# A scheduler that counts visits of small matrix products later, and copies that may go to either of two engines

## The chip, the cores and the metric

The kernel runs on one core of a Trainium2 chip. The metric is the device time of one execution in microseconds (us). The engines are TensorE (PE, with its weight loads as PEld), VectorE (DVE), ScalarE (ACT), GpSimd (POOL) and SyncE (SP, which issues the transfers). TensorE runs at one of two clocks, 1.2 or 2.4 GHz; the profile calls the granted clock 0.50 or 1.00.

## What is computed

An attention with a state that is updated token by token (batch 4, 8 heads, 768 tokens, head size 48), followed by two feed-forward layers over 3072 tokens of width 384:

```python
k_n = k / (norm(k) + 1e-6)
for t in range(S):                      # S = 768
    y[t] = q[t] @ state
    state = state + beta[t] * outer(k_n[t], v[t] - k_n[t] @ state)
x = y as 3072 x 384
x = ((x @ w_a) * (x @ w_b)) @ w_out     # width 1536
h = x @ w_in                            # width 2048
out = (max(h, 0) + alpha * min(h, 0)) @ w_out2
```

## The kernel before, in words

The attention works on six chunks of 128 tokens (c = 0 to 5), each of two steps of 64 tokens (j = 0, 1). For a chunk, small products on TensorE make the grams of keys and queries (tile `g`), VectorE inverts a triangular matrix in a long row of small operations (`inv`, `itmp`), two more stages of small products complete the inverse (`w`, and `xx` in the first chunk), and each step is then a chain: `rp` (what the state already holds), a subtraction on VectorE, `up`, copies of `up` into `SU`, `sp`, the new state from `sp`, and `yp`, the output. ScalarE and VectorE split `yp` into a high and a low half in `x`, from which the large products of the feed-forward layers start (`p` and `o` in the first layer, `h` and `o` in the second, each 128x512). The small products are fp32, and so each counts as two TensorE instructions in the trace; the large ones use split fp32r operands, three passes each.

Nothing is issued in the order of the Python code. A `Recorder` notes every operation, a `Schedule` lays them out, and `emit` issues them in that order; the trace therefore shows line 203 for all of them. `Schedule.run` is a list scheduler. It keeps a planned time `free` for each engine and `ready` for each task; consecutive small products form one task, each large product is a task of its own. At each turn it takes the engine that can start first, and on it the task of highest `level` among those that can start within `SLACKS` of that time (0.25 us on TensorE). The plan fixes the order on every engine; the true times follow from the chip. `plan` makes four such runs with different levels and keeps the one whose planned end is earliest.

"The front" is all that TensorE does ahead of the first large product. There, gaps in TensorE's plan are filled with dummy products, `spin`, 128x512 each, that depend on nothing but a cleared tile; `spins` lists them and gets a `None` once the first large product is placed. The inner loop puts in spins from the end of the last task while this holds:

```python
each = SPIN if fast(at) else 2 * SPIN          # SPIN = 0.227
if at + each > b - REST - 0.08 * (b - free[e]) or len(spins) == len(s.spins):
    break                                      # REST = 0.25, 200 spins at hand
```

where `b` is the planned start of the next task. Their number is thus fixed when the kernel is built, and on the chip TensorE goes through all of them before it comes to the product behind them, whether that product's operands are there or not. An operation recorded on `nc.evict` may go to ScalarE or VectorE: ScalarE is tried first, and VectorE takes it where ScalarE's plan is more than `BUSY` = 1.5 us behind, or where it is the earlier by the plan (the function `when`).

The first chunk's copies of `up` into `SU` (in `step`, lines 960 to 965) go to ScalarE for x = 0 and to VectorE for x = 1; in later chunks all of them go to ScalarE. Both copies of one half read the same PSUM tile.

Of the kernel before, what the change touches and what calls it, by code (L numbers as in the profile page):

```python
# [125 lines left out]
PE_, ACT_, DVE_, POOL_, SP_ = range(5)  # L126
# [76 lines left out]
            getattr(s.engines[op.eng], name)(*(real(x) for x in op.a), **{w: real(x) for w, x in op.k.items()})  # L203


HOP, SAME, LATE, BEGIN = 0.15, 0.03, 1.0, 1.3
ENTER, LEAVE = 0.2, 0.19
BUSY = 1.5
TURNS = 4
# [35 lines left out]
class Schedule:  # L245
# [105 lines left out]
    def run(s, level):  # L351

        tasks = s.tasks
        waits = [len(t.before) for t in tasks]
        ready, start, end = ([0.0] * len(tasks) for _ in range(3))
        open_ = [[t.n for t in tasks if not waits[t.n] and any(w[0] == e for w in t.ways)] for e in range(5)]
        free, port, link, was = [BEGIN] * 5, 0.0, 0.0, False
        rows = [None] * 5
        landed, order, spins = [], [], []
        chunk, spans = {"at": 0, "next": 0.0}, []  # L360
        clock = {"w": 0, "fast": False}
        warm = s.of[min(s.spins[0].before)]

        def fast(b):
            while (clock["w"] + 1) * WINDOW <= b:
                w = clock["w"]
                busy = sum(k * (min(y, (w + 1) * WINDOW) - max(x, w * WINDOW)) for x, y, k in spans if y > w * WINDOW and x < (w + 1) * WINDOW)
                spans[:] = [x for x in spans if x[1] > (w + 1) * WINDOW]
                clock["fast"] = busy >= WINDOW * (KEEP_UP if clock["fast"] else RISE)
                clock["w"] = w + 1  # L370
            return clock["fast"]

        def ask(b):
            chunk["next"] = b + next(x for y, x in FETCH if link > b + y)

        def fetched(b, cost, n):
            at, late = chunk["at"], 0.0
            for x in range(at, at + n):
                if x == STOCK - CHUNK:
                    ask(b)  # L380
                if x >= STOCK and (x - STOCK) % CHUNK == 0:
                    now = b + late + cost * (x - at) / n
                    late += max(0.0, chunk["next"] - now)
                    ask(max(now, chunk["next"]))
            chunk["at"] = at + n
            return late

        def when(n, e):
            at, first = max(ready[n], free[e]), tasks[n].ways[0][0]
            return at if e == first or free[first] > at + BUSY else max(at, free[first] + 0.01)  # L390

        while len(order) < len(tasks):
            at, e = min((min(when(n, e) for n in open_[e]), e) for e in range(5) if open_[e])
            n = max((n for n in open_[e] if when(n, e) <= at + SLACKS[e]), key=lambda n: (tasks[n].ways[0][0] == e, level[n], -n))
            t = tasks[n]
            for w in t.ways:
                open_[w[0]].remove(n)
                if w[0] == e:
                    t.go(w)
            order.append(n)  # L400
            b = max(ready[n], free[e])
            cost, lag = t.cost, t.lag
            if e in (ACT_, DVE_, POOL_):
                if rows[e] == t.rows:
                    b = max(ready[n], free[e] - (0.12 if e != DVE_ else 0.1))
                rows[e] = t.rows
            if t.port:
                wait = max(0.0, port - b - 0.1)
                port = b + wait + t.lag - 0.05
                cost, lag = cost + wait, lag + wait  # L410
            if e == PE_:
                if not spins or spins[-1] is not None:
                    at = max(free[e], end[warm] if end[warm] else 1e9)
                    while True:
                        each = SPIN if fast(at) else 2 * SPIN
                        if at + each > b - REST - 0.08 * (b - free[e]) or len(spins) == len(s.spins):
                            break
                        spins.append(at)
                        at += each
                        spans.append((at - each, at, 1))  # L420
                        fetched(at - each, each, 2)
                    if t.large:
                        spins.append(None)
                if t.large == was:
                    b += ENTER if not t.large else LEAVE
                    spans.append((b - 0.2, b, 1))
                was = not t.large
                if not fast(b):
                    cost += t.cost
                    lag += t.cost  # L430
                late = fetched(b, cost, 2 if t.large else 4 * len(t.ops))
                cost, lag = cost + late, lag + late
                spans.append((b, b + cost, 1 if t.large else LIGHT))
            if t.dma:
                if e == SP_:
                    if len(landed) >= 8:
                        b = max(b, landed[-8])
                    landed.append(0)
                link = max(b + 1.5, link) + lag
                end[n] = link + 0.55 + (LATE if link > 45 else 0)  # L440
                if e == SP_:
                    landed[-1] = end[n]
            else:
                end[n] = b + lag
            start[n] = b
            free[e] = b + cost
            for m in t.after:
                u = tasks[m]
                if u.before[n]:
                    r = b + 1e-6  # L450
                elif u.eng == e == PE_:
                    r = b + cost
                else:
                    r = end[n] + (SAME if u.eng == e and not t.dma else HOP)
                ready[m] = max(ready[m], r)
                waits[m] -= 1
                if not waits[m]:
                    for w in u.ways:
                        open_[w[0]].append(m)
        s.start, s.end = start, end  # L460
        for t in tasks:
            t.ops[0].eng = t.eng
        s.first = min(start[t.n] for t in tasks if t.large)
        ops = [(start[n], n, op) for n in order for op in tasks[n].ops]
        ops += [(at, 0, op) for at, op in zip((x for x in spins if x is not None), s.spins)]
        return [op.n for _, _, op in sorted(ops, key=lambda x: x[:2])]
# [90 lines left out]
class Attention:  # L557
# [50 lines left out]
    def bank(s, name, tag="chain"):  # L608
        return s.pools[tag].tile([128, 512], F32, tag=tag, name=name, bufs=BANKS[tag])
# [283 lines left out]
    def step(s, c, j, L, mates=(), joined=False, wide=False):  # L893
# [6 lines left out]
        nc, ap = s.nc, s.ap  # L900
# [3 lines left out]
        def mate():  # L904
            m = mates.pop(0) if mates else None
            return none if m is None else m()
# [3 lines left out]
        SU, SN = s.SU[st % 2], s.SU[(st + 1) % 2]  # L910
# [21 lines left out]
        if st > 0:  # L932
# [12 lines left out]
            for x in range(2):  # L945
                sl, other = slice(64 * x, 64 * x + 64), slice(64 - 64 * x, 128 - 64 * x)
                got = rp[1][other, 0 : second.stop - second.start]
# [4 lines left out]
        for group in (uneven if mates else halves,) if wide else ((h,) for h in halves):  # L952
            ups = [bank("up") for _ in group]
            beside, keep = mate()
            turned = group is uneven
            for n, i, o in dealt(group, beside):
                for x in range(2):
                    sl, at = slice(64 * x, 64 * x + 64), 64 * (x ^ n ^ turned)
                    nc.tensor.matmul(ups[n][at : at + 64, i, :], s.TT[sl, j, o, :], R[sl, o, :], start=True, stop=True)
            for n, (_, hs) in enumerate(group):  # L960
                for x in range(2):
                    at = 64 * (x ^ n ^ turned)
                    got = ups[n][at : at + 64, 0 : hs.stop - hs.start]
                    (nc.scalar if c or not x else nc.vector).copy(SU[x][64 * x : 64 * x + 64, hs, 0:48], got)
                    s.spend(ACT, 1.9)
            keep()
            yield
        for group in (halves,) if wide and not mates else ((h,) for h in halves):
# [4 lines left out]
            for i in range(8):  # L973
                for n, (o, _) in enumerate(group):
                    for x in range(2):
                        sl, at = slice(64 * x, 64 * x + 64), 64 * (x ^ n)
                        nc.tensor.matmul(sps[n][at : at + 48, i, :], bk[sl, j, o + i, :], SU[x][sl, o + i, 0:48], start=True, stop=True)
                beside(i)
            for n, (_, hs) in enumerate(group):
                for x in range(2):  # L980
                    at, old, new = 64 * (x ^ n), slice(64 - 64 * x, 112 - 64 * x), slice(64 * x, 64 * x + 48)
# [11 lines left out]
        for o, _ in halves:  # L993
            for x in range(2):
                rows, at = slice(0, (112, 128)[x]), (o // 4 + x) * 64
                for n in range(4):
                    for q in range(4):
                        kk, h, e, start, stop = s.BLOCKS[q][n]
# [15 lines left out]
def attn_moe_kernel(tc, kt, qt, kn, vn, beta, w_a, w_b, w_o, w_in, w_o2, alpha, out):  # L1014
    nc = tc.nc
    with ExitStack() as ctx:
# [383 lines left out]
        for c in range(NSC):  # L1400
# [3 lines left out]
            if c > 0:  # L1404
                N = A.load(c + 1) if c + 1 < NSC else None
                if c == 1:
                    run(moe, WAIT)
                    pools["out"] = Pool(rec, second, (p0,), 1, True)
                    going = run(moe, AHEAD) and going
# [213 lines left out]
```

## Time and profile before

| | us |
|---|---|
| median of 3 runs (lowest, highest) | 1011.08 (1008.9, 1012.37) |
| the profiled execution's own time | 1012.1 |
| its span, first to last instruction | 1010.1 |
| TensorE busy in the span | 993.7 (98%) |
| first large product starts at | 75.34 |

The profiled execution is 0.1% above the median, and 2.0 us of its time lie outside of its span. TensorE's share of 98% counts the spins as work, and the ends of products are modelled by the profile.

### The profile page before, as it was taken

The numbers are of one execution on the slowest core, as the hardware profiler recorded it, in microseconds if no ns is written. First come the engines' busy times: TensorE is split into PE (matmuls) and PEld (weight loads), VectorE is DVE, ScalarE is ACT, GpSimd is POOL, SyncE is SP. The second block draws the span as 40 slices with busy tenths as digits, with TensorE's granted clock in tenths as the row PEclk, the third lists the DMA queues.
The fourth block names the chain that finished last, engine by engine and source line by source line (L and its number), as shares of the span: only waits on it lengthen the run. The fifth ranks groups of instructions, "written<-read, shape, count | busy, mean of one in ns | idle before, by whom it ended". The sixth has DMA issues, their size and how long they took to land.

```text
span 1010.1 us, 22391 instructions
## 1 busy us (share of the span) xinstructions
PE 993.7 (98%) x9388; PEld 813.3 (81%) x9388; DVE 631.5 (63%) x1260; ACT 445.7 (44%) x804; POOL 499.0 (49%) x406
## 2 busy tenths in 40 slices
PE   8989999999999999999999999999999999999998
PEld 6777777888888788788878888888888888888886
DVE  7789997865895687678677778343343343433333
ACT  5846774454545454545578785121121221211211
POOL 4557864653565366456468875333333333333332
PEclk8889999999999999999999999999999999999999
DMA  9536432002201210000035542010020010000100
GB/s 201 210 96 230 141 89 81 32 4 65 94 1 32 65 65 1 18 18 32 16 97 167 165 133 84 1 31 32 1 63 1 1 63 0 32 1 1 32 1 31
DMA packets 27076, 61.31 MB, mean 61 GB/s; under 512 B 4320, under 2 KB 8928, under 8 KB 26976
## 3 DMA queue, kind: packets, MB, share of 16 engines
q1 hardware_dynamic: 26544, 59.50, 19.5%
q8 instruction: 73, 1.20, 0.5%
q10 hardware_dynamic: 432, 0.39, 0.1%
q14 instruction: 27, 0.22, 0.1%
HBM read 50.44 MB, written 9.44 MB: 59 GB/s over the span
## 4 chain that ended last, share of the span: by engine, by line
PE 92%; POOL 2%; DMA 2%; issue 2%; DVE 1%; ACT 0%; DVEq 0%; POOLq 0%; SPq 0%
PE o L203 33%; PE p L203 27%; PE h L203 19%; PE g L203 3%; PE yp L203 2%; DMA Z<-in_qt_dram 2%; PE spin L203 2%; PE up L203 2%; POOL W L203 2%; PE sp L203 1%; PE rp L203 1%; PE w L203 1%; POOL wu L203 1%; DVE raw L203 0%; DVE inv L203 0%
## 5 line engine op out<-in xcount | busy, mean ns | idle before, releaser
L203 PE MATMUL p<-x,wu 128*128 128x512 f32 x1296 | 318.4, 394 | 2.3 <-DVE x L203 1.5
L203 PEld LDWEIGHTS p<-x,wu 128*128 128x128 f32 x1296 | 240.1, 188 | 55.6 <-issue 3.6
L203 POOL TENSOR_TENSOR g<-neg,g 128x512 fp32r<-128x512 f32 x95 | 124.5, 1311 | 261.0 <-ACT g L203 258.5
L203 POOL TENSOR_TENSOR wu<-W,wu 128x384 fp32r<-128x384 f32 (+1 forms) x126 | 176.4, 1404 | 112.6 <-ACT wu L203 112.6
L203 DVE TENSOR_SCALAR neg<-h,al 128x512 f32<-128x512 f32 (+1 forms) x97 | 72.3, 745 | 227.9 <-PE h L203 225.2
L203 PE MATMUL o<-g,v 128*128 128x512 f32 x870 | 211.5, 388 | 0.0
L203 PE MATMUL h<-x,v 128*128 128x512 f32 x864 | 211.3, 389 | 0.0
L203 ACT CAST g<-neg 128x512 fp32r<-128x512 f32 (+1 forms) x97 | 59.7, 616 | 305.6 <-DVE neg L203 280.3
L203 PEld LDWEIGHTS o<-g,v 128*128 128x128 f32 x870 | 162.4, 188 | 33.8 <-ACT g L203 0.4
L203 PEld LDWEIGHTS h<-x,v 128*128 128x128 f32 x864 | 162.1, 188 | 33.8 <-DVE neg L203 0.2
L203 PE MATMUL o<-g,wu 128*128 128x512 f32 x648 | 163.9, 393 | 1.3 <-ACT g L203 1.1
L203 PEld LDWEIGHTS o<-g,wu 128*128 128x128 f32 x648 | 120.6, 188 | 28.3 <-ACT g L203 1.5
L203 ACT CAST wu<-W 128x768 fp32r<-128x768 f32 (+1 forms) x144 | 96.8, 676 | 57.3 <-PE p L203 38.1
L203 POOL TENSOR_TENSOR g<-a,g 128x512 fp32r<-128x512 f32 x57 | 80.0, 1403 | 56.6 <-ACT g L203 56.6
L203 ACT COPY a<-p 128x512 f32<-128x512 f32 x72 | 42.2, 587 | 95.4 <-PE p L203 66.2
L203 DVE TENSOR_TENSOR inv<-inv,itmp 128x110 f32<-128x110 f32 (+12 forms) x256 | 75.0, 293 | 8.9 <-ACT eu L203 0.9
L203 DVE SCALAR_TENSOR_TENSOR neg<-h,neg 128x512 f32<-128x512 f32 (+1 forms) x97 | 66.5, 686 | 3.3
L203 PE MATMUL g<-Z 48*64 48x64 f32 (+1 forms) x1024 | 63.3, 267 | 3.9 <-DMA Z<-in_kt_dram 1.5
L203 PEld LDWEIGHTS g<-Z 48*64 48x64 f32 x1024 | 47.8, 150 | 12.3 <-issue 4.9
L203 DVE TENSOR_TENSOR a<-p,a 128x512 f32<-128x512 f32 x59 | 40.6, 688 | 25.1 <-PE p L203 24.1
L203 DVE TENSOR_TENSOR itmp<-inv,gd 128x96 f32<-128x96 f32 (+8 forms) x150 | 40.7, 271 | 6.1 <-ACT gd L203 1.4
L203 POOL TENSOR_TENSOR f<-f,v 128x384 int32<-128x384 int32 x32 | 36.5, 1156 | 10.0 <-DVE v L203 10.0
(111 smaller groups left out, 940.6 us busy)
## 6 DMA issues: line engine op xcount, KB each, us to landing
v<-in_w_o_dram SPq DMA_DIRECT2D x16, 384.0 KB, 3.2
v<-in_w_in_dram SPq DMA_DIRECT2D x16, 384.0 KB, 3.6
Z<-in_kt_dram SPq DMA_DIRECT2D x24, 192.0 KB, 3.8
Z<-in_qt_dram SPq DMA_DIRECT2D x24, 192.0 KB, 3.8
v<-in_vn_dram SPq DMA_DIRECT2D x12, 384.0 KB, 3.2
x2d<-x2s SPq DMA_DIRECT2D x18, 256.0 KB, 2.4
xf<-x2d SPq DMA_DIRECT2D x18, 256.0 KB, 2.8
raw<-in_w_a_dram SPq DMA_DIRECT2D x11, 384.0 KB, 5.2
```

Source lines behind the costliest of these rows:

```text
L203: getattr(s.engines[op.eng], name)(*(real(x) for x in op.a), **{w: real(x) for w, x in op.k.items()})
```

## The change

Two constants are added. In the front, every task of small products gets a planned start that is 0.7 us later (`FRONT`), ahead of the loop that fills the gap with spins. Behind the first large product, a task of small products counts as ready 0.4 us later (`CARE`) when the scheduler looks for what to place next; its planned start, once it is taken, isn't changed. And the first chunk's copies of `up` for x = 1 are recorded on `evict` in place of VectorE, those for x = 0 on `evict` in place of ScalarE.

```diff
-HOP, SAME, LATE, BEGIN = 0.15, 0.03, 1.0, 1.3
+HOP, SAME, LATE, BEGIN, CARE = 0.15, 0.03, 1.0, 1.3, 0.4
+FRONT = 0.7
...
         def when(n, e):
-            at, first = max(ready[n], free[e]), tasks[n].ways[0][0]
+            late = CARE if e == PE_ and spins and spins[-1] is None and not tasks[n].large else 0.0
+            at, first = max(ready[n] + late, free[e]), tasks[n].ways[0][0]
             return at if e == first or free[first] > at + BUSY else max(at, free[first] + 0.01)
...
             if e == PE_:
+                if (not spins or spins[-1] is not None) and not t.large and at > 1:
+                    b += FRONT
                 if not spins or spins[-1] is not None:
...
                     got = ups[n][at : at + 64, 0 : hs.stop - hs.start]
-                    (nc.scalar if c or not x else nc.vector).copy(SU[x][64 * x : 64 * x + 64, hs, 0:48], got)
+                    (nc.scalar if c else nc.evict).copy(SU[x][64 * x : 64 * x + 64, hs, 0:48], got)
```

No operation is added or removed by name; the order on every engine and the number of spins are what the scheduler makes of it.

## Rows read from the trace of the kernel before

**Rows 1.** The page, busy time, share and count of each engine

```profile
PE 993.7 (98%) x9388; PEld 813.3 (81%) x9388; DVE 631.5 (63%) x1260; ACT 445.7 (44%) x804; POOL 499.0 (49%) x406
```

**Rows 2.** Busy time in stretches: length, then each engine, clock, DMA share, GB/s

```profile
0.00:75.30 75.30, 66.09 (x1422) 54.95 (x1422) 59.05 (x130) 44.99 (x79) 38.92 (x53) 0.84 0.61 168
75.30:122.60 47.30, 44.94 (x192) 35.65 (x192) 44.00 (x110) 32.50 (x45) 38.36 (x23) 1.00 0.57 190
171.20:537.60 366.40, 366.40 (x4689) 297.81 (x4689) 270.01 (x658) 196.34 (x367) 202.49 (x163) 1.00 0.13 40
```

**Rows 3.** TensorE's waits from 75 to 125 us: total, times, longest

```profile
PE p L203 <- DVE x L203: 1.5, 1, 1.5
PE o L203 <- ACT g L203: 1.1, 1, 1.1
PE p L203 <- ACT a L203: 0.9, 1, 0.9
```

**Rows 4.** Busy time in the front's two stretches at half clock

```profile
17.00:34.10 17.10, 15.02 (x205) 13.16 (x207) 15.66 (x44) 9.93 (x15) 8.06 (x12) 0.50 1.02 318
64.80:71.60 6.80, 6.80 (x140) 6.14 (x143) 4.54 (x9) 2.63 (x7) 4.67 (x3) 0.50 0.24 63
```

**Rows 5.** Timeline of TensorE, the last grams and the stage behind them

```profile
20.39 6.40 PE L203 MATMUL g<-Z 48*64 48x64 f32 x106 [0.48 <-DMA Z<-in_qt_dram]
27.46 3.04 PE L203 MATMUL g<-Z 48*64 48x64 f32 x52 [0.68 <-issue]
...
40.51 1.15 PE L203 MATMUL g<-Z 48*64 48x64 f32 x32
41.59 7.34 PE L203 MATMUL spin<-still 128*128 128x512 f32 x31
48.86 1.29 PE L203 MATMUL w<-hw,ef 32*32 32x32 f32 x128
```

**Rows 6.** Timeline of VectorE and ScalarE beside it

```profile
40.64 2.07 DVE L203 STREAM_TRANSPOSE hw<-inv 128x1024 f32<-128x1024 f32 x1
...
42.40 1.21 ACT L203 ACTIVATE Z<-g 64x512 f32<-64x512 f32 x2
...
50.22 1.78 DVE L203 COPY hw<-w 32x256 f32<-32x256 f32 x4 [5.63 <-PE w L203]
```

**Rows 7.** Timeline of TensorE, from there to the last step of the front

```profile
52.42 1.12 PE L203 MATMUL xx<-TT,hw 32*32 32x32 f32 x108 [0.59 <-issue]
...
55.88 1.60 PE L203 MATMUL up<-v,TT 64*64 64x48 f32 x47 [0.78 <-issue]
...
59.48 2.00 PE L203 MATMUL yp<-Z,SU 112*32 112x64 f32 x128
...
63.16 0.92 PE L203 MATMUL rp<-SU,Z 48*64 48x48 f32 x49 [0.95 <-issue]
...
64.93 3.65 PE L203 MATMUL up<-v,TT 64*64 64x48 f32 x64
...
70.52 2.50 PE L203 MATMUL yp<-Z,SU 112*32 112x64 f32 x128
```

**Rows 8.** The copies of `up`, 50 to 75 us: count, busy, mean ns, idle

```profile
L203 ACT COPY SU<-up 64x384 f32<-64x384 f32 x4 | 1.9, 472 | 7.7 <-PE up L203 6.3 <-DVE SU L203 1.3
L203 DVE COPY SU<-up 64x384 f32<-64x384 f32 x4 | 2.2, 561 | 1.9 <-ACT SU L203 1.9
```

**Rows 9.** Timeline of TensorE, small products between large ones

```profile
127.61 1.51 PE L203 MATMUL w<-TT,hw 32*64 32x64 f32 x64
...
130.88 1.41 PE L203 MATMUL rp<-SU,Z 48*64 48x48 f32 x64
...
511.20 1.15 PE L203 MATMUL rp<-SU,Z 48*64 48x48 f32 x64
```

**Rows 10.** Timeline of TensorE and VectorE, the second block's start

```profile
171.25 1.98 PE L203 MATMUL p<-x,wu 128*128 128x512 f32 x8
...
170.96 1.07 DVE L203 TENSOR_TENSOR x<-yp,x 128x256 fp32r<-128x256 f32 x3
```

## The prediction

> **What bounds the kernel now.** I read the page's busy shares first [rows 1]: TensorE is busy for 98% of the span, so only its work, or the time in which it lacks work, can move the end. The stretches come second [rows 2]. From 171 us to 538 us TensorE is busy without a gap, with attention and first layer together, and the second layer behind it holds no small product, so neither constant is read there. What is left is the front, 75.3 us up to the first large product at 75.34, and the stretch from there to 171 us. The spins count as busy time, so the front's 66.09 us of busy time say nothing of what it must cost. I therefore read the timeline of TensorE in the front against those of ScalarE and VectorE, one small group after the other, and asked of each: was it the operands that came last, or TensorE?
>
> At the front's widest place it was TensorE. After the last grams it runs 31 spins, from 41.59 to 48.86, and then `w` [rows 5]. `w` needs the transposed inverse `hw`, which VectorE ended at 40.64 + 2.07 = 42.71, and PSUM that ScalarE cleared of the last gram at 42.40 + 1.21 = 43.61 [rows 6]. So `w` could have begun at about 43.65, and began 5.2 us later; VectorE stood idle for 5.63 us until it came. The plan had placed these 31 spins so that they would end before `hw` was there; TensorE came to them late, because it took longer over the grams than planned.
>
> Behind `w` it is a mixture. Three groups stop in their midst for 0.59, 0.78 and 0.95 us with "issue", a wait for nothing that the profile shows [rows 7]; elsewhere the copies on ScalarE and VectorE come last by some tenths. And the clock is at 1.2 GHz from 17.0 to 34.1 and from 64.8 to 71.6 [rows 4], at an exact half of the full clock. Behind the first large product TensorE waits for 1.5, 1.1 and 0.9 us [rows 3]. Waits inside small groups don't show as idle time, since the ends of products are modelled: they show as longer groups. An undisturbed `rp` of 64 takes 1.15 us [rows 9]; the one at 130.88 takes 1.41.
>
> **FRONT, up to `w`.** Per task, 0.7 us more of planned time. Where the gap was zero, the spin rule leaves room for 0.7 - 0.25 - 0.06 = 0.39 us, which is one spin of 0.227 at full clock and none at half clock. Where there was a gap already, nearly all of the 0.7 is filled: 0.92 x 0.7 / 0.227 = 2.8 spins. A spin takes 7.34 / 31 = 0.237 us on the chip [rows 5]. That decides the sign. The planned time of `w` is set by VectorE's inverse, not by TensorE. If five gram groups that run back to back (158 products, 32 each, the first two of rows 5) each take 0.7 us of the plan and are filled with at most 0.23, the gap ahead of `w` loses 5 x 0.7 us of spins and gets 5 x 0.23 back elsewhere: -2.3 us. Against it stand `w`'s own 0.7 (+0.65 filled) and the key grams ahead of the inverse, which come one or two visits later in the plan and so move the planned inverse by 0.7 to 1.4 us (+0.65 to +1.3). I take -1.0 for the start of `w`. Bounds: it can't come more than 5.2 us earlier, since its operands aren't there, and if the grams are filled as fully as the others it comes some 3 us later.
>
> **FRONT, from `w` to the first large product.** By the code these are 15 tasks: `w` and `xx` two each, then `up`, `up`, `sp`, `sp`, `yp`, `rp`, `up`, `up`, `sp`, `sp`, `yp`. Some 8 wait in the plan and get up to 3 spins more, 7 follow another and get one: 8 x 3 x 0.237 + 7 x 0.237 = 7.3 us more work in TensorE's queue. It is a chain, so uncovered it would all be lost. Cover: the three stops of "issue", 0.59 + 0.78 + 0.95 = 2.3 us, if what they wait for comes at its own time; an estimated 1.2 us in which TensorE waits for copies ahead of a group (half of the three stops); as a choice 1.5 us, about what the 7 single spins cost, where the second half of `up` or `sp` or the `yp` runs beside the copies that the chain needs. And the clock: at 1.2 GHz `up` took 3.65 us for 64, where 47 at full clock took 1.60, or 2.2 for 64; `yp` took 2.50 against 2.00 [rows 7]; with a half-clock `sp` beside them about 2.4 us in all. The fall at 64.8 comes behind the stretch with the longest stop, 0.95 us in `rp`; more spins ahead of `rp` fill just that stretch. 2.3 + 1.2 + 1.5 + 2.4 = 7.4, so I take -0.1. Bounds: all of the clock lost, and each spin in that stretch at double length, gives +5; half as many spins gives -3.
>
> The Trainium skill, "TensorE: Matmul & The Clock Gate", section "A second HAM failure mode: psum-queue depth-cycling", says that short idle times between groups of products are enough to let the clock swing between its levels. The trace agrees so far that the clock fell at 64.8 behind stops that were all below 1 us [rows 4, 7]. By that rule, denser spins would hold 2.4 GHz through both stretches; that is the first rival below.
>
> **The copies.** The two copies of a half read one PSUM tile, and they run one after the other: VectorE waits for ScalarE's twice, 1.9 us in sum, and ScalarE for VectorE's once, 1.3 us [rows 8]. So two on ScalarE, 0.472 + 0.472, take the place of 0.472 + 0.561: -0.09 for each of the four halves, two of them on the chain, -0.2. Bounds: -0.6, as the 1.3 us wait in front of the last copy goes, and +0.6 if ScalarE has decoding work in front of them.
>
> The Trainium skill, "Trainium Architecture — The Big Picture", section "The five engines, in one table", warns against simple elementwise work on ScalarE and calls VectorE up to about three times as fast per element. By that, four copies would lengthen by up to 0.56 x 2 = 1.1 us each, 2.2 us on the chain; for these copies out of PSUM the rows say the reverse, 472 ns on ScalarE against 561 on VectorE, and the measurement decides.
>
> **Behind the first large product.** The wait of 1.5 us for `x` [rows 3] comes from VectorE's own order (steps of the next inverse ahead of the split); I leave it at 0, with -1.5 and +1 as bounds. Those of 1.1 and 0.9 follow from decoding of weights on ScalarE, VectorE and GpSimd; a plan nearer to the chip puts some of it into the 5.63 us in which VectorE stood idle: -0.4, bounds -2 and +1. CARE makes the scheduler place one or two more large products (0.23 us each) ahead of a small group that is only just ready. It costs nothing where large products are at hand, and they are. It removes waits inside groups: for `w` at 127.61 and `rp` at 130.88 about 0.3 us each [rows 9], some 1.2 us over the chunk: -0.7. From the second chunk on there are none to remove. Its price is a later chain: the second block's first `p` began at 171.25, while VectorE's split of `x` ran from 170.96 to 172.03 [rows 10], so there is about 1 us of slack, and nine links by 0.4 us are 3.6 us. Half of the links have slack of their own, so +0.2; bounds 0 and +2.6.
>
> **The sum.** -1.0 - 0.1 - 0.2 + 0 - 0.4 - 0.7 + 0.2 = -2.2 us. Against the profiled execution, 1012.1 (span 1010.1 and 2.0 around it), that is 1009.9; as the median lies 1.0 lower, 1008.9 on its scale. About 0.3%, 3 us, is what a measurement of this kernel can tell from no change, so that is "the same".
>
> **Rivals.** (1) The clock holds. At 2.4 GHz the five cold gram groups would take 5 x 1.15 = 5.8 in place of 9.4 us [rows 5], and the seven spins among them half of their 3.4; that alone brings `w` to the bound of 5.2 us, less 0.7 for its own visit, and 2.4 us come from the second stretch: -6.9, with the other terms about 1003.5. For it: both falls stand behind stops. Against it: in the first stretch TensorE waits for transfers, at a DMA share of 1.02 [rows 4], and spins only fill that where the plan knows of the wait. (2) The spins ahead of `w` fall from 31 to about 12, the grams being spread out in the plan: -4.5, the rest as in the sum: 1005. For it: the idle 5.63 us. Against it: all gaps already filled are filled again. (3) The other side: the front's chain takes its new spins uncovered. It decides as soon as fewer than about 3 us of the 7.3 are covered; then +4.3 and more: 1015.5. For it: every spin is issued whether needed or not, and `w` is late today for that very reason. (4) The chunk's chain becomes too late for the second block: +2.6 on top of the rest without CARE's gain, 1012.5. (5) The plan comes out nearly as before, 1011.
>
> **Chances.** The sum's case 0.46 (a fifth of it beyond -3 us, its own range 1006 to 1011.5), (1) 0.09, (2) 0.18, (3) 0.15, (4) 0.07, (5) 0.05. Faster by over 0.3%: 0.09 + 0.09 + 0.18 = 0.36. Slower: 0.13 of (3) and 0.01 of (4), 0.14. The same: 0.50. The range leaves out most of (1) and the far end of (3): 1003.5 to 1014.5.
>
> **What would show it.** The run of spins ahead of `w` shorter than 31, and `w` a microsecond earlier; VectorE's idle time there below 5.6; more than 100 spins in all; "issue" stops in `xx`, `up`, `rp` smaller; clock 1.00 from 64.8 to 71.6; the first large product at 74 to 75; `SU` copies of the first chunk on ScalarE; `w` and `rp` of the second chunk at 1.15 us; no new wait of `p` at 171. I am wrong if the first large product moves by more than 3 us either way, or if TensorE waits for `x` at a block's start.

## The result and the profile after

| | before | after |
|---|---|---|
| median, us (lowest to highest) | 1011.37 (1008.9 to 1012.65), 5 runs | 1017.76 (1015.64 to 1019.98), 5 runs |
| ratio of the times (95% interval) | | 1.0073 (1.0056 to 1.0089) |
| profiled execution, its span, us | 1012.1, 1010.1 | 1016.97, 1015.2 |
| mean granted clock of the profiled execution | 0.988 | 0.987 |

The change makes the kernel 0.7% slower, about 6.4 us by the medians. The forecast was 1008.9 us and "the same"; the median lies outside of its range. Medians and ratios here leave out slow runs, such as one of 1225.7 us at a mean granted clock of 0.75 in the first experiment.

The page after, the busy times of the engines:

```profile
PE 1003.7 (99%) x9412; PEld 817.1 (80%) x9412; DVE 624.6 (62%) x1260; ACT 449.3 (44%) x808; POOL 497.1 (49%) x402
```

TensorE is busy for 10.0 us more than in [rows 1], and its share went up: the page alone would pass for an improvement. Most of it is spins: 102 of them in place of 78 (their counts in the timeline of the front, added up), and more of them at half clock. So the stretches come next, with the columns of [rows 2]:

```profile
0.00:83.00 83.00, 76.55 (x1446) 59.47 (x1447) 61.94 (x138) 47.85 (x84) 42.24 (x56) 0.84 0.52 150
83.00:128.30 45.30, 44.97 (x192) 35.52 (x192) 40.59 (x98) 31.88 (x44) 34.88 (x19) 1.00 0.61 210
178.10:543.60 365.50, 365.50 (x4683) 296.71 (x4683) 264.40 (x655) 193.94 (x362) 197.72 (x156) 1.00 0.13 39
18.90:36.00 17.10, 17.10 (x190) 13.62 (x187) 15.68 (x42) 10.72 (x16) 7.38 (x11) 0.50 1.03 349
56.40:66.60 10.20, 9.34 (x163) 7.44 (x164) 6.95 (x10) 4.10 (x9) 4.13 (x4) 0.50 0.14 40
```

The first large product starts at 83.00 in place of 75.34, 7.7 us later; the span is 5.1 us longer, so 2.6 us come back behind it. The second half-clock stretch lies at 56.4 to 66.6, earlier and longer than that of [rows 4]. The timeline of TensorE in the front says where the 7.7 us are (in brackets the idle time ahead of the instruction and what ended it):

```profile
20.52 1.97 PE L203 MATMUL g<-Z 48*64 48x64 f32 x32
...
28.40 1.97 PE L203 MATMUL g<-Z 48*64 48x64 f32 x32
30.30 0.79 PE L203 MATMUL spin<-still 128*128 128x512 f32 x1
31.03 1.97 PE L203 MATMUL g<-Z 48*64 48x64 f32 x32
32.93 3.95 PE L203 MATMUL spin<-still 128*128 128x512 f32 x10
...
47.25 3.92 PE L203 MATMUL spin<-still 128*128 128x512 f32 x16
51.10 0.75 PE L203 MATMUL w<-hw,ef 32*32 32x32 f32 x64
51.78 0.49 PE L203 MATMUL spin<-still 128*128 128x512 f32 x1
52.67 0.75 PE L203 MATMUL w<-hw,ef 32*32 32x32 f32 x64 [0.39 <-ACT hw L203]
...
55.63 0.24 PE L203 MATMUL xx<-TT,hw 32*32 32x32 f32 x2 [0.44 <-ACT TT L203]
57.26 1.07 PE L203 MATMUL xx<-TT,hw 32*32 32x32 f32 x62 [1.39 <-DVE TT L203]
...
58.99 1.95 PE L203 MATMUL up<-v,TT 64*64 64x48 f32 x32
60.86 0.79 PE L203 MATMUL spin<-still 128*128 128x512 f32 x1
61.59 1.95 PE L203 MATMUL up<-v,TT 64*64 64x48 f32 x32
...
71.56 1.15 PE L203 MATMUL rp<-SU,Z 48*64 48x48 f32 x64
...
83.00 1.17 PE L203 MATMUL p<-x,wu 128*128 128x512 f32 x4 [0.61 <-DVE x L203]
```

Start of `w`: 51.10 against 48.86, +2.2. From `w` to `rp`: 20.5 us against 12.6 (61.42 - 48.86 before), +7.9. From `rp` to the first large product: 11.4 against 13.9, -2.5.

The second term is where the loss sits. `w` and `xx` are now each two groups of 64 with a spin between, and the second group of each waits: 0.39 us for ScalarE's copy of `hw`, 0.44 and 1.39 for the copies of `TT`. In the longest of these waits, at 56.4, the clock falls to 1.2 GHz; each half of `up` takes 1.95 us (47 products took 1.60 in [rows 7], so 32 some 1.1) and each spin 0.79 (0.49 ahead of the fall). What VectorE does beside it:

```profile
51.93 0.42 DVE L203 COPY hw<-w 32x256 f32<-32x256 f32 x1 [6.47 <-PE w L203]
...
54.91 0.87 DVE L203 COPY hw<-w 32x256 f32<-32x256 f32 x2
55.81 0.95 DVE L203 TENSOR_REDUCE ss<-sq 128x16 f32<-128x768 f32 x1
56.79 0.42 DVE L203 COPY TT<-xx 32x256 f32<-32x256 f32 x1
```

The two halves of `xx` write the same two PSUM tiles, each half its own rows. With planned time between them, the scheduler puts a copy of the first half ahead of the second half's products, and these wait until it is done (56.79 + 0.42 = 57.21, and they go on at 57.26); the copy in turn stands behind a reduction of 0.95 us. The plan itself sees no wait there, since the kernel's `Recorder` counts two operations on a tile as dependent only where their rows and columns overlap. In [rows 6] the four copies of `hw` came in one row, after both halves of `w`. VectorE's idle time ahead of them grew from 5.63 to 6.47 us. At full clock TensorE's groups are as fast as before (`yp` 2.00 us both times): what changed is the order, the number of spins and where the clock falls.

### The profile page after: what moved, and what is told of

It reads as the page before. It is cut to its first block, busy times and chain, and to the rows that moved or that the text cites. A ratio compares the mean times of both kernels' runs of the same rounds, so it can differ in the third digit from the quotient of the medians.

```text
span 1015.2 us, 22431 instructions
## 1 busy us (share of the span) xinstructions
PE 1003.7 (99%) x9412; PEld 817.1 (80%) x9412; DVE 624.6 (62%) x1260; ACT 449.3 (44%) x808; POOL 497.1 (49%) x402
## 4 chain that ended last, share of the span: by engine, by line
PE 95%; DMA 2%; DVE 1%; ACT 1%; SPq 0%; issue 0%; DVEq 0%; ACTq 0%
PE o L203 34%; PE p L203 29%; PE h L203 19%; PE g L203 3%; PE spin L203 2%; PE yp L203 2%; PE up L203 2%; DMA Z<-in_kt_dram 1%; PE sp L203 1%; PE w L203 1%; PE rp L203 1%; DMA raw<-in_w_o_dram 1%; SPq L203 0%; DVE hw L203 0%; ACT W L203 0%
## 5 line engine op out<-in xcount | busy, mean ns | idle before, releaser
L203 POOL TENSOR_TENSOR wu<-W,wu 128x768 fp32r<-128x768 f32 (+1 forms) x125 | 180.0, 1444 | 144.9 <-ACT wu L203 137.9
L203 PE MATMUL o<-g,wu 128*128 128x512 f32 x648 | 166.7, 395 | 0.0
L203 POOL TENSOR_TENSOR g<-a,g 128x512 fp32r<-128x512 f32 x54 | 74.2, 1374 | 36.5 <-ACT g L203 36.5
L203 ACT CAST g<-a 128x512 fp32r<-128x512 f32 x59 | 36.5, 619 | 9.5 <-DVE a L203 8.8
```

## The experiments

None of these kernels leaves out or changes part of the computation; spins compute nothing that is used. "Ratio" is that to the kernel before, run beside it on the same chip, with its 95% interval. "Mean clock" is the granted clock of a whole run, and a kernel's is the mean over its runs. Plans are made by the scheduler, so a one-line edit can move many instructions; for that reason several of them cut one thing in different ways.

**The change without FRONT.**

```diff
-FRONT = 0.7
+FRONT = 0.0
```

> The changed kernel with FRONT = 0, so with CARE and the copies alone. Theory A, the front's added spins are the whole loss: the first large product at about 75 us in place of 83, the 2.6 us won behind it kept, so about 1008 to 1010. Theory B, later visits behind the front or copies on one engine cost something too: 1013 or more.

Measured: 0.9982 (0.9971 to 0.9992), 1007.37 us. CARE and the copies together gain 0.2%.

**FRONT alone.** CARE is 0.0 and the copies are as before.

> The kernel before with FRONT = 0.7 alone (CARE = 0, copies as before). Theory A: the first large product at about 83 us. If CARE made the 2.6 us behind the front, they are missing here and the time is about 1019 to 1020; if the better plan that follows from FRONT made them, 1017.

Measured: 1.0072 (1.0048 to 1.0095), 1017.14 us. FRONT is the whole loss. Its six runs also show what the clock is worth: two with a mean granted clock of 0.994 to 0.995 took 1011.2 and 1011.7 us, those at 0.985 to 0.987 from 1017.0 to 1018.3. It is one program, so its time depends on the clock. So does that of the kernel before, but less: on the same chip its runs at 0.994 and 0.996 took 1008.9 and 1009.3 us, those at 0.987 1011.5 and 1013.4. FRONT costs about 2 us at the higher clock and about 5 at the lower. Its profile is of the run with 1011.2 us; timeline of TensorE, and its one stretch at half clock:

```profile
49.20 0.24 PE L203 MATMUL xx<-TT,hw 32*32 32x32 f32 x2 [0.44 <-ACT TT L203]
50.84 1.07 PE L203 MATMUL xx<-TT,hw 32*32 32x32 f32 x62 [1.39 <-DVE TT L203]
```

```profile
49.90:60.10 10.20, 9.26 (x163) 7.23 (x163) 7.46 (x11) 3.08 (x7) 4.09 (x4) 0.50 0.14 40
```

The same waits as in the changed kernel, and the clock falls in the same one. What is missing is the stretch at half clock among the grams: here `w` starts at 44.67, in the changed kernel's profile at 51.10. The stage from `w` to `rp` is as long as there, 19.2 us.

**CARE alone**, and **the copies alone**. The first edit is against the changed kernel, the second against the kernel before.

```diff
-FRONT = 0.7
+FRONT = 0.0
...
-                    (nc.scalar if c else nc.evict).copy(SU[x][64 * x : 64 * x + 64, hs, 0:48], got)
+                    (nc.scalar if c or not x else nc.vector).copy(SU[x][64 * x : 64 * x + 64, hs, 0:48], got)
```

```diff
-                    (nc.scalar if c or not x else nc.vector).copy(SU[x][64 * x : 64 * x + 64, hs, 0:48], got)
+                    (nc.scalar if c else nc.evict).copy(SU[x][64 * x : 64 * x + 64, hs, 0:48], got)
```

> The kernel before with CARE = 0.4 alone. If CARE makes the gain behind the front, the waits inside small groups from 122 to 150 us are gone and the time is 1 to 2 us below before, 1008; if the copies on one engine make it, it is that of before, 1009.6.

> The kernel before with the copies on evict alone. By the prediction 0.2 us; if they and not CARE made the gain of the kernel without FRONT, 2 us, so 1007.5.

Measured: CARE 1.0005 (0.9989 to 1.0022), nothing; the copies 0.998 (0.9963 to 0.9997), 2.0 us by the point value (0.3 to 3.7 by the interval). So the gain of the first experiment is most likely that of the copies.

**The change's order without its lone spins.** Runs of spins of length one are dropped from the finished plan (18 of 102); every other instruction stays in its place.

```diff
-        return best[1]
+        spin, order = {op.n for op in s.spins}, best[1]
...
+        drop = {n for run in runs if len(run) == 1 for n in run}
+        return [n for n in order if n not in drop]
```

> The changed kernel with its finished order, only that the 18 spins that stand alone between two small groups are dropped when the instructions are issued. Theory A, the spins themselves cost (0.43 us each at full clock and 0.75 at half clock, by the distance from group to group): first large product at 75 to 77 us, about 1010. Theory C, the order that FRONT makes of copies and groups on the other engines costs: first large product at 81 or later, 1015 or more.

Measured: 1.0026 (1.0012 to 1.0039), 1012.18 us. In this order the lone spins cost 4.8 us (1.0073 - 1.0026). Without them it is still slower than before, with half clock from 53.6 to 63.8 in its profile; the mean clock of its runs is 0.987, that of the kernel before beside it 0.992.

**The order before with lone spins.** The counterpart: the plan before, and one spare spin wherever two groups of small products adjoin in the front (96 spins).

> The kernel before with its finished order on all engines, only that one spin is put between small groups that follow one another in the front (17 spins; 78 become about 95). Theory S1, the spin between joined groups is the cost by itself, 0.43 us each at full clock and 0.75 at half: 6 us or more over before. Theory S2, what costs is the order that FRONT gives the copies between the halves: within 2 us of before.

Measured: 1.0002 (0.9989 to 1.0015), 1011.25 us, mean clock of its runs 0.996. The same kind of spin that costs 4.8 us in the new order costs nothing on balance in the old one. Timeline of TensorE, and below it the stretch from `w` to `rp`:

```profile
51.11 0.75 PE L203 MATMUL xx<-TT,hw 32*32 32x32 f32 x64
51.79 0.49 PE L203 MATMUL spin<-still 128*128 128x512 f32 x1
52.21 0.75 PE L203 MATMUL xx<-TT,hw 32*32 32x32 f32 x64
```

```profile
47.90:62.30 14.40, 14.05 (x528) 10.85 (x527) 11.23 (x19) 7.87 (x19) 4.93 (x6) 1.00 0.11 31
```

The second half of `xx` waits for nothing, although a spin stands ahead of it as in the changed kernel. The clock stays at 1.00 through that stretch, which takes 14.4 us (12.6 before, also at 1.00; 20.5 after).

That the balance is even does not make the spins free: they buy clock. The kernel before, beside it, has a mean clock of 0.990. At one clock the two differ: this kernel's two runs at 0.991 took 1014.3 and 1014.9 us, those of the kernel before at 0.991 to 0.992 from 1009.5 to 1011.3. So the lone spins cost about 4 us here too, and its other nine runs, at 0.995 to 0.998, win that back; none of the 23 runs of the kernel before came above 0.993.

**FRONT only where the plan has a gap already.**

```diff
-                if (not spins or spins[-1] is not None) and not t.large and at > 1:
+                if (not spins or spins[-1] is not None) and not t.large and at > 1 and ready[n] > free[e]:
```

> The changed kernel with FRONT counted only where the plan has TensorE wait for the operands of a small group; groups that follow one another without a wait stay joined, with no spin between. 97 spins in the front, against 102 changed and 78 without FRONT. Theory S, splitting joined groups is what costs: first large product at 73 to 76 us, 1007 to 1010. Theory Q, any added spin costs its 0.237 us: 19 more than without FRONT, 4.5 us, so 1012.

Measured: 0.9984 (0.997 to 0.9998), 1009.66 us; by its trace it has 106 spins, not the 97 of the expectation, which was a miscount. With more spins than the changed kernel, none of them lone, it is 0.9% faster than it. The whole loss belongs to the groups that followed another without a gap; where TensorE waits anyhow, 0.7 us of planned time cost nothing, and against 0.9982 without FRONT they win nothing.

**FRONT on all, but not on a second half that writes the tile of the group just ahead.** This joins the halves of `w` and `xx` again; `room` holds the tiles that TensorE's last task wrote.

```diff
-                if (not spins or spins[-1] is not None) and not t.large and at > 1:
+                if (not spins or spins[-1] is not None) and not t.large and at > 1 and not room & {id(op.dst.tile) for op in t.ops}:
                     b += FRONT
...
                 was = not t.large
+                room = {id(op.dst.tile) for op in t.ops}
```

> The changed kernel with FRONT as it is, except for the second halves of w and of xx, which write the PSUM tiles of the first halves. They stay joined to them, as before; all other groups keep the spin between (104 spins). Theory S3, the order of copies between those halves is the main loss (their waits, and the half clock behind them): no wait for TT or hw, no half clock from 50 to 60 us, w to rp in 14 to 16 us in place of 20.5, and the ratio falls from 1.007 to 1.000 to 1.002. Theory S4, the other single spins and the longer gaps are: 1.005 or more, the half clock still there.

Measured: 1.0046 (1.0029 to 1.0063), 1015.21 us. The stretch from `w` to `rp` in its windows, and rows of its timeline:

```profile
51.50:66.00 14.50, 13.64 (x528) 10.55 (x527) 12.60 (x23) 8.18 (x21) 9.35 (x10) 1.00 0.11 31
```

```profile
51.54 1.29 PE L203 MATMUL w<-hw,ef 32*32 32x32 f32 x128
...
54.11 1.33 PE L203 MATMUL xx<-TT,hw 32*32 32x32 f32 x128
...
77.71 4.36 PE L203 MATMUL p<-x,wu 128*128 128x512 f32 x18 [0.44 <-DVE x L203]
```

The waits inside `w` and `xx` are gone, the clock holds, and the stretch falls from 20.5 to 14.5 us. That settles where these waits come from. By the ratios 2.7 of the 7.4 us come back (1.0073 and 1.0046, times 1011; the two intervals overlap a little, so the 2.7 are loose), fewer than the 6 us of the two profiles. `w` still comes at 51.5. What comes back goes with the clock, whose mean is 0.991 here and 0.986 in the changed kernel; and at a clock like that of the kernel before beside it (0.992) this kernel is still 4.7 us slower, with 17 lone spins.

**Twice the size.** `FRONT = 1.4`, 172 spins.

> The changed kernel with FRONT = 1.4: four spins and not one between groups that follow one another. If the loss is the queue of spins, the first large product comes at 90 us or later and the time is above 1024. If part of the loss is the half clock that thinly filled groups bring, the clock stays at 1.00 over nearly all of the front here and gives some of it back: 1019 to 1023.

Measured: 1.0072 (1.0053 to 1.0091), 1019.35 us. Its front, the columns as above:

```profile
6.80:84.60 77.80, 75.18 (x1501) 57.53 (x1499) 63.97 (x163) 45.97 (x85) 40.70 (x49) 1.00 0.50 156
```

The clock is at 2.4 GHz from the first grams to the first large product, and that product still starts at 84.66. The clock is won, and the longer queue of spins eats it.

**Planned later, without filling.** FRONT is added behind the spin loop, so the plan is later, but no spin goes there; some 16 spins remain.

> The changed kernel with FRONT added behind the loop of spins: the plan has the small groups 0.7 us later, but no spin fills that time; 18 spins in the front. If the later plan by itself is harmless and the spins cost, the first large product comes at 72 to 75 us although more of the front runs at half clock, 1008 to 1011. If spins are needed for the clock and for the stops of issue, the groups run at half clock up to the end of the front: 1012 or more.

Measured: 1.0113 (1.0099 to 1.0128), 1022.64 us, mean clock 0.968. Timeline of TensorE:

```profile
54.51 0.95 PE L203 MATMUL w<-hw,ef 32*32 32x32 f32 x53 [1.05 <-ACT hw L203]
...
76.65 3.65 PE L203 MATMUL up<-v,TT 64*64 64x48 f32 x64 [5.00 <-DVE v L203]
...
88.83 1.60 PE L203 MATMUL p<-x,wu 128*128 128x512 f32 x5 [3.78 <-DVE x L203]
```

This is the slowest of all: a later plan with hardly a spin in it, and TensorE at half clock in most of the front. So leaving the spins out doesn't give back what FRONT costs.

**The spins ahead of `w` cut.** Last spins of the longest run dropped from the finished plan: 20 of 31 in the kernel before, 10 of 31 in the change without FRONT, 10 of 19 in the kernel with FRONT in gaps only.

> The kernel before with its finished order, only that 20 of the 31 spins ahead of w are dropped. If the spins alone held w back, it starts at about 44.2 us in place of 48.86, when its operands come, and the first large product at 70 to 71 us: 1007. If something else binds there (the copies behind w, or a lower clock for want of spins), w comes earlier and the first large product by less than 2 us.

> The changed kernel with FRONT = 0 and 10 of the 31 spins ahead of w dropped: 2.3 us earlier than without the cut if w waits for spins alone, ratio 0.996 against before; if the spins pay for themselves through clock and issue, 0.998 as without the cut.

> The kernel of FRONT in gaps alone, with 10 of the 19 spins ahead of w dropped. If w still waits for spins and not for its operands there, w and the first large product come 2.3 us earlier, 1007.5 on the scale of that run (ratio 0.996); if the clock falls for want of them, no gain.

Measured: 1.0009 (0.9992 to 1.0025), 0.9972 (0.9959 to 0.9985) and **0.996** (0.9945 to 0.9975), the last at 1006.73 us the fastest kernel of this study, ahead of both versions. The intervals of the last two overlap those of the kernels that they were cut from (0.9982 and 0.9984), so the cut's own share isn't settled. The kernel before with 20 spins fewer, timeline of TensorE:

```profile
36.85 2.81 PE L203 MATMUL spin<-still 128*128 128x512 f32 x11
42.70 1.87 PE L203 MATMUL w<-hw,ef 32*32 32x32 f32 x128 [3.04 <-DVE hw L203]
...
69.64 0.24 PE L203 MATMUL yp<-Z,SU 128*32 128x64 f32 x1 [3.21 <-issue]
```

`w` comes 6.2 us earlier and now waits for its operand, so the reading of [rows 5, 6] was right: the run of spins set its start, the inverse comes next. Not all of the 6.2 us are the cut's, though: in this execution the grams were at half clock only from 25 to 28.7 us, and the run of spins began at 36.85 in place of 41.59. All 31 spins from there would have ended at about 44.2 (an estimate, 36.85 + 7.34), so the cut itself brought 1.5 us here. And `w` takes 1.87 us in place of 1.29, since the clock fell here (42.5 to 52.7), and a stop of "issue" of 3.21 us stands in `yp`. The first large product starts only 4.1 us earlier, at 71.26, and by the medians nothing is won: the mean clock of its runs is 0.987, that of the kernel before beside it 0.992.

## Why the prediction was wrong

**FRONT, from `w` to the first large product: the step that failed.** I put 7.3 us of new spins against 7.4 us of cover, -0.1; the profile shows +5.4 (+7.9 to `rp`, -2.5 behind it). I treated the edit as spins in a fixed order, with the clock as a credit of 2.4 us. The cover by the stops of "issue" mostly came: 2.3 us of them became 0.64. The credit for the clock did not: the clock fell earlier and for longer, 10.2 us against 6.8. It fell in a wait that none of my terms held: the planned gap changed the order of the copies on ScalarE and VectorE, and two halves that share their PSUM tiles began to wait for each other's copies (0.39, 0.44 and 1.39 us). With the halves joined, the waits and this fall are gone, and in that profile the same term is 77.71 - 51.54 = 26.2 us against 26.5 before: -0.3, near what I put. The sign was that of the third rival, which priced the case nearly right (1015.5 against 1017.8) for a reason that holds in part: at one clock the lone spins cost about 4 us, in the old order too, but there they hold the clock and pay for themselves. The rest goes with the clock, which is 0.986 in the changed kernel's runs and 0.990 to 0.992 in those of the kernel before.

**FRONT, up to `w`: -1.0 predicted, +2.2 measured.** The run ahead of `w` fell from 31 to 16, as the step said, but the gaps ahead of the last four grams were filled by as many more: in the timelines 7, 4, 3, 5 and 31 spins became 10, 8, 7, 9 and 16, 50 both times, and they and the four grams take 18.2 us against 18.4. The four lone spins between the grams from 20.52 on come on top. I priced one at up to 0.23; they run at half clock, where one takes 31.03 - 28.40 = 2.63 us from group to group, against 6.40 x 32 / 106 = 1.93 without a spin [rows 5]: 0.7 each, 2.8 in all. A stop of "issue" of 0.68 us [rows 5] is covered by them, which makes 2.1; measured from 20.52 to 32.93 are 12.4 us against 10.0 in the profile before (from 20.39 to the end of the gram at 27.46), 2.4 more. It hangs on the clock that this stretch has in a run: in the profile of FRONT alone, at 1.00 throughout the grams, `w` comes 4.2 us earlier than before. In the joined version's profile `w` is late by 2.7 us; how much of the 4.7 us that this version still loses to the kernel before is this, and how much the other lone spins, no run separates.

**The first rival.** Dense spins do hold the clock: 1.00 through the whole front with 1.4 us. The Trainium skill, "TensorE: Matmul & The Clock Gate", section "A second HAM failure mode: psum-queue depth-cycling", says that short idle times between groups make the clock swing. The traces agree: in the stretch from `w` on it fell behind waits of at most 1.39 us, and held there in the joined version, where those waits were gone. But a held clock was no gain in itself, since the spins that hold it stand in the same queue (84.66 us to the first large product).

**The second rival.** "`w` earlier by 4.5 us" was put at a gain of 6 us in all. Cutting 20 spins brought `w` to its operands, at 42.70, and 1.0009 in time. The spins that looked like waste also held the clock: without them it fell at 42.5, and the runs' mean went from 0.992 to 0.987.

**The copies: right in sign, mis-sized.** -0.2 predicted, -2.0 measured alone. Two copies back to back on ScalarE, by form from 50 to 85 us after, against [rows 8]:

```profile
L203 ACT COPY SU<-up 64x384 f32<-64x384 f32 x8 | 3.8, 473 | 3.2 <-PE up L203 3.1
```

All eight went to ScalarE at 473 ns, and the waits of one engine for the other, 1.9 and 1.3 us, are gone. I had counted only the difference of two durations. That these waits make the difference isn't shown: the interval starts at 0.3 us, and the mean clock of these runs is 0.992 against 0.990 of the kernel before beside them. The warning that I weighed, from the Trainium skill, "Trainium Architecture — The Big Picture", section "The five engines, in one table", that VectorE is up to about three times as fast for such work, isn't borne out for these copies: 561 ns on VectorE [rows 8] against 473 on ScalarE.

**Behind the first large product.** TensorE's waits from 83 to 130 us are now

```profile
PE p L203 <- DVE x L203: 0.6, 1, 0.6
PE p L203 <- ACT a L203: 0.2, 1, 0.2
```

2.7 us fewer than in [rows 3]. I had put 0.4 there, within the bounds. Such waits differ from plan to plan (by the profiles 1.1 us in the change without FRONT, 3.1 with CARE alone), so I put them to no single edit.

**CARE: the mechanism right, its worth about nothing.** The waits inside groups are gone, as said (`w` and `rp` of the second chunk took 1.51 and 1.41 us in [rows 9], and 1.52 and 1.42 with FRONT and no CARE; the copies alone, without CARE, shorten them too, to 1.16 and 1.25), and the second block's first large product doesn't wait for `x`; timeline of TensorE:

```profile
133.06 1.16 PE L203 MATMUL w<-TT,hw 32*64 32x64 f32 x64
...
138.68 1.15 PE L203 MATMUL rp<-SU,Z 48*64 48x48 f32 x64
...
178.08 2.21 PE L203 MATMUL p<-x,wu 128*128 128x512 f32 x8
```

-0.5 net was predicted and can't be told from 1.0005 (0.9989 to 1.0022). The fourth rival, the chain too late for the second block, did not happen.

**The sum.** The two terms of FRONT were predicted at -1.1 and came to +7.7 in the profile, in which what the copies gave in the front is already counted; the waits behind came out 2.3 better. The forecast fell with the assumption that the order of the work, and with it the clock, stays as good as before.

## What to carry to other kernels

A constant in a list scheduler isn't priced by the idle time that it inserts: any gap between two groups is an invitation to place something there, so ask what will be placed, and whether the second group writes a tile that the first group's reader still holds. Planned slack where the plan already waits is harmless (0.9984 against 1.0073 here). When two engines copy out of one tile by turns, time a version with one engine (0.998 here). Dummy work that keeps the clock up has a price of its own where the engine would not wait anyhow, so compare runs at one clock before calling it free; a long run of it in front of a stage may still be paying for itself, and cutting it has to be timed.

## What the runs showed of the hardware

The clock differs between runs of one program, and with it the time by 6 us (1011.2 at a mean clock of 0.995, 1017.0 and more at 0.985 to 0.987), as much as the whole change does. That the stretch among the grams makes this difference is read from one profile at each level, not shown for the other runs.

The stops of "issue" on TensorE stand at fixed places of its instruction stream: in the fronts of all these profiles they come after 221, 347, 730, 858, 985, 1113, 1368 or 1495 products, within two, whatever the plan (spins counted; the steps are 126 to 128, or two or three times that). Their length isn't fixed: after 1113 products 0.95 us before and 0.64 in the changed kernel, after 1368 none in these two, 1.18 us without FRONT and 3.21 with 20 spins cut. What ends them the profile doesn't show.
